# Token mixing of the first batch by one pair's 128 channels, with the first order, the merged order and the loads found anew

## The chip, the cores and the metric

The kernel runs on one core of a Trainium2 chip. The metric is the time of one execution on the device, in microseconds. The engines in play are TensorE (PE in the profile, with PEld for its weight loads), VectorE (DVE), ScalarE (ACT), GpSimd (POOL, which issues the loads) and SyncE (SP, which issues the first loads, the turning transfers and the stores).

## The reference

Attention with a sliding window of 128 and 4 sink positions, then a mixer: over tokens, then over channels.

```python
scores = scale * np.matmul(q, k.transpose(0, 1, 3, 2))       # 4 batches, 8 heads, 768 positions, 64 dims
is_sink = pos[None, :] < int(n_sink)
rel = pos[:, None] - pos[None, :]
keep = is_sink | ((rel >= 0) & (rel < int(window)))
scores = np.where(keep, scores, -1000000000.0)
...
x = np.ascontiguousarray(attn_out.transpose(0, 2, 1, 3)).reshape(B, S, H * D)     # 4 x 768 x 512
xt = x.transpose(0, 2, 1)
h = np.maximum(xt @ w_tok1, 0.0) @ w_tok2                     # 768 -> 256 -> 768, per channel
u = x + h.transpose(0, 2, 1)
h2 = np.maximum(u @ w_ch1, 0.0) @ w_ch2                       # 512 -> 1536 -> 512, per token
return (u + h2).astype(np.float32)
```

## The kernel before

*Units of work.* Two heads make a pair p; a batch b has four pairs (128 channels each), so there are 16 pairs, 0 to 15. q and k of a pair are turned (dims on the partitions): for pairs 0 to 7 by TensorE (`turn`, L473, and `transposed`, L491), for pairs 8 to 15 by a turning transfer that SP issues (`turned_by_dma`, L417). Scores of a pair are made in three groups g of two key tiles each (`scores`, L543), the exponential is ScalarE's (L583). What lies outside the window is removed in one of two ways. Either `masked` (L528) first writes -32768 into the bank by a matmul of the identity with a mask, so that the exponential gives zero; or VectorE multiplies the exponentials with a 0/1 mask afterwards (`mask`, L588). Batch 0 uses the first way for the (p, g) in `MASKED_BY_PE` (L69), which is all of its twelve groups but one. `pv` (L630) multiplies with the values, and VectorE takes the reciprocal and normalizes into x_sb.

*Token mixing* works on a group of channels (`group`, L733): here 256, so two groups, of two pairs each, per batch. `mix_h` (L752) makes relu(x w_tok1) for a group, with w_tok tiles as weights and 256 columns of x_sb streaming. `mix_u` (L780) makes the second product; the x that is added to it is either added by VectorE (L797) or, with `by_pe`, by a matmul of the identity into the same bank, after which ScalarE or VectorE copies. `transpose_u` (L862) turns u for batch 0 on TensorE in blocks of 128 x 128. In batch 0, mix_h takes one 128-row part at a time, and mix_u and transpose_u take two of the six token tiles.

*Channel mixing* of batch b (`mix_channels`, L968): 24 units v1(ft, half) of four matmuls of 384 columns each, whose weights are w_ch1 tiles and whose streaming operand is the turned u (uT); then for each of the six token tiles four `out_part` units of three 512-wide matmuls with w_ch2, an addition on VectorE (L1003) and a store. The first v1 unit of a half needs uT of all four pairs.

*The order* is set when the program is built, by a planner (class Plan, L266). It walks through three lists with estimated costs. FIRST_BATCH (L54) is the order of batch 0's attention and token mixing on TensorE, by short names: q0/k0 turns, m00 masks, s00 scores (pair, group), x1 sink scores, o00 values, h, u, t the token mixing. The main list is the channel mixing of all batches. The side list is the attention and token mixing of the next batch; MERGED (L47) gives, as n/m, which side unit n stands behind how many main units m. LOADS (L59) is the order in which GpSimd issues loads: v, q, k of a pair, T and A for w_tok1 and w_tok2, C0 to C3 for the quarters of w_ch1, D0 to D3 for those of w_ch2. Every engine then runs its own list in this order. q, k, v and weights are converted from float32 by the transfer. The planner keeps one estimate of the transfer queue (`queue`, L269), eight loads may be under way (LANES), and a turning transfer adds its `bulk` to the queue (L368). PSUM has two double banks for scores (ps_sc) and four banks for all else (ps_mx).

Of the kernel before, what the change touches and what calls it, by code (L numbers as in the profile page):

```python
# [10 lines left out]
BF16 = mybir.dt.bfloat16  # L11
# [5 lines left out]
def kernel(  # L17
# [15 lines left out]
    P = 128  # L33
# [13 lines left out]
    MERGED = (  # L47
# [5 lines left out]
    )  # L53
    FIRST_BATCH = (  # L54
        "q0 k0 m00 m01 s01 s00 q1 k1 m02 s02 m10 x1 s10 m11 q2 s11 o00 o01 m12 k2 s12 m20 s20 q3 m21 k3 s21 "
        "m22 o11 s22 o10 s30 x3 m31 h01 m32 s31 s32 o20 o21 h00 o30 o31 u02 u00 u04 h10 h11 t00 t02 t04 u10 "
        "u12 u14 t10 t12 t14"
    )
    LOADS = (  # L59
        "v1 v2 T0 v3 A0 q4 k4 v4 C0 C1 q5 k5 v5 q6 C2 q7 C3 k6 k7 D0 q8 D1 k8 v6 D2 D3 q9 v7 k9 q10 q11 k10 "  # L60
        "v8 k11 q12 v9 q13 v10 k12 k13 v11 k14 q14 q15 k15 v12 v13 v14 v15"
    )
# [5 lines left out]
    U_BY_DMA = [(2, 0), (2, 1), (3, 0), (3, 1)]  # L68
    MASKED_BY_PE = [(p, g) for p in range(NHP) for g in range(NT // 2) if (p, g) != (NHP - 1, 0)]  # L69

# [195 lines left out]
    class Plan:  # L266
        def __init__(self):
            self.free = {"PE": 0.0, "ACT": 0.0, "DVE": 0.0, "SP": 0.0, "POOL": 0.0}
            self.queue, self.landings = 0.0, []  # L269
# [69 lines left out]
        def run(self, first, main, side):  # L339
# [5 lines left out]
            while any(first) or main or side or self.pending:  # L345
# [13 lines left out]
                if o is not None and (t is None or o[0] <= t):  # L359
                    op = self.pending.pop(o[1])  # L360
                    op.fn(o[2])
                    self.free[o[2]] = o[0] + op.cost[o[2]]
                    op.done = self.free[o[2]] + op.lag
                    if op.loads:
                        self.queue = max(self.queue, self.free[o[2]] + FIRST) + op.lag
                        op.done = self.queue + LAND
                        self.landings += [op.done] * op.loads
                    elif op.bulk:  # L368
                        self.queue = max(self.queue, self.free[o[2]]) + op.bulk
                        if op.stores:  # L370
                            op.done = self.queue + LAND
                    continue
# [360 lines left out]
    def group(b, g):  # L733
        return g * DM // 2, DM // 2

# [5 lines left out]
    def u_part(b, g, s0, n):  # L741
        return tiles["mix", b][1].rearrange("p (g t c) -> p g t c", g=2, t=NT)[:, g, s0:s0 + n]

# [117 lines left out]

    def transpose_u(b, g, s0, n):  # L862
        ct0, nct = group(b, g)[0] // P, group(b, g)[1] // P
# [7 lines left out]
        w = nct * n * P  # L871
        op = Op(
            {"ACT": 190.0 + 0.78 * w, "DVE": 150.0 + 0.52 * w},
            lambda e: copy(
                e, tiles["mix", b][2].rearrange("c (g t k p) -> c g k t p", g=2, t=NT, p=P)[:, g, :, s0:s0 + n],
                tiles["ps_ut", b, g, s0].rearrange("c k (t p) -> c k t p", p=P),
            ),
        )
        op.urgent = 1 + g
        for half in range(s0 // QH, (s0 + n - 1) // QH + 1):  # L880
            done.setdefault(("uT", b, half), []).append(op)
        return unit(nct * n * 56, run, [done["u", b, g, s0]], {"mx": [[op]]}, [op])

    def first_attention():


        for p in range(NHP):
            prepare(p)
        made = {}
# [277 lines left out]
```

## Time and profile before

| | us |
|---|---|
| median of 3 runs (201.4 to 201.74) | 201.64 |
| profiled execution | 201.1 |
| its span | 199.3 |
| TensorE busy | 190.9 |
| ScalarE busy | 106.1 |
| VectorE busy | 99.7 |

How to read it: a profile row of a group has source line, engine, operation, output<-inputs, sizes and count, then busy time and the mean length of one in ns, then the idle time of the engine just before such an instruction and what ended it. A timeline row has start and length in us. Matmuls are pipelined: the length of one includes its fill, and the pace is read from the distance between starts. A transfer row gives the time from issue to landing. Line numbers of the changed kernel are lower by one to higher by four, depending on the place.

### The profile page before, as it was taken

Reading aid. Unit: us, or ns where it says so; the run is one execution under the profiler, and the core shown is the slowest. Engines: PE = TensorE matmul, PEld = TensorE weight load, DVE = VectorE, ACT = ScalarE, POOL = GpSimd, SP = SyncE. Lnnn points to the kernel's source line nnn. Section 1 sums busy time; section 2 is a strip of 40 time slices with the busy share of each in tenths; the row PEclk is TensorE's granted clock in tenths of the full one; section 3 lists DMA queues with packets and bytes.
Section 4 is the critical chain, followed back from the end, with each engine's and each line's share of the span. In section 5 each row is a group of like instructions: output and inputs, shape, how many; then the busy total and the mean of one; then the engine's idle time right before and its main releaser. Section 6 shows DMA issues by size and latency. Waiting matters only on the chain.

```text
span 199.3 us, 4761 instructions
## 1 busy us (share of the span) xinstructions
PE 190.9 (96%) x1997; PEld 114.6 (58%) x2015; DVE 99.7 (50%) x215; ACT 106.1 (53%) x185; POOL 67.9 (34%) x86
## 2 busy tenths in 40 slices
PE   6699999999999999999999999999999999999992
PEld 2355885566565665556556755656557746564452
DVE  4777763857867465326367676604235721001222
ACT  4899658988626225868556284776401106771000
POOL 6299869787547723648420000000000000000000
PEclk9999999999999999999999999999999999999999
DMA  6999999999999999999999845100021191000223
GB/s 205 291 258 185 168 183 171 176 183 180 162 150 131 169 150 226 148 208 151 158 155 165 204 103 135 54 2 3 0 99 62 32 230 53 3 0 9 96 109 105
DMA packets 92358, 26.28 MB, mean 132 GB/s; under 512 B 82352, under 2 KB 89392, under 8 KB 92336
## 3 DMA queue, kind: packets, MB, share of 16 engines
q0 software_dynamic: 67232, 11.80, 79.1%
q1 hardware_dynamic: 25104, 14.17, 32.2%
q8 instruction: 16, 0.26, 0.5%
q14 instruction: 6, 0.05, 0.1%
HBM read 26.75 MB, written 6.29 MB: 166 GB/s over the span
## 4 chain that ended last, share of the span: by engine, by line
PE 92%; DMA 3%; ACT 1%; issue 1%; SPq 1%; DVE 0%
PE ps_mx L135 83%; PE ps_sc L135 7%; DMA k_f<-in_k_dram 3%; PE ps_mx L483 1%; PE ps_sc L499 1%; SPq L107 1%; PE ps_mx L138 1%; PE ps_mx L471 0%; ACT pT L583 0%; ACT u_sb L142 0%; DVE k_bf L144 0%; ACT kT L142 0%; DVE o_sb L1041 0%
## 5 line engine op out<-in xcount | busy, mean ns | idle before, releaser
L135 PE MATMUL ps_mx<-w_ch,v1T 128*128 128x512 bf16 (+2 forms) x297 | 65.9, 362 | 0.9 <-issue 0.2
L135 PE MATMUL ps_mx<-uT,w_ch 128*128 128x384 bf16 x384 | 65.8, 326 | 0.0
L148 ACT ACTIVATE v1T<-ps_mx 128x384 bf16<-128x384 f32 x80 | 39.3, 492 | 26.7 <-PE ps_mx L135 14.2
L583 ACT ACTIVATE pT<-ps_sc 128x1024 bf16<-128x1024 f32 (+1 forms) x48 | 44.1, 951 | 12.9 <-PE ps_sc L135 11.6
L135 PEld LDWEIGHTS <-w_ch 128*128 128x128 bf16 x384 | 36.1, 98 | 24.1 <-DVE x_sb L693 0.5
L135 PEld LDWEIGHTS <-v1T 128*128 128x128 bf16 x312 | 28.3, 98 | 26.6 <-issue 0.2
L1003 DVE TENSOR_TENSOR o_sb<-ps_mx,u_sb 128x512 f32<-128x512 f32 x23 | 15.9, 689 | 38.3 <-PE ps_mx L135 32.4
L120 POOL DMA_DIRECT2D q_bf<-in_q_dram x24 | 19.8, 830 | 10.2 <-PE ps_mx L135 2.7
L120 POOL DMA_DIRECT2D k_bf<-in_k_dram x24 | 19.7, 826 | 5.3 <-DMA k_bf<-in_k_dram 3.0
L135 PEld LDWEIGHTS <-w_tok 128*128 128x128 bf16 x192 | 18.1, 98 | 4.8 <-issue 0.5
L128 POOL DMA_DIRECT2D v_aug<-in_v_dram x16 | 16.5, 1037 | 12.4 <-PE ps_mx L135 5.7
L150 DVE TENSOR_SCALAR v1T<-ps_mx 128x384 bf16<-128x384 f32 x16 | 8.8, 553 | 19.8 <-PE ps_mx L135 19.7
L797 DVE TENSOR_TENSOR u_sb<-ps_mx,x_sb 128x512 bf16<-128x512 f32 x21 | 13.8, 687 | 7.6 <-PE ps_mx L135 7.5
L135 PEld LDWEIGHTS <-pT 128*128 128x128 bf16 x352 | 14.5, 98 | 3.8 <-issue 0.3
L135 PE MATMUL ps_mx<-v_aug,pT 128*128 128x65 bf16 x352 | 15.7, 194 | 0.0
L148 ACT ACTIVATE h1T<-ps_mx 128x512 bf16<-128x512 f32 (+1 forms) x9 | 4.5, 503 | 20.8 <-PE ps_mx L135 20.7
L135 PE MATMUL ps_sc<-qT,kT 64*64 64x192 bf16 (+3 forms) x288 | 14.7, 249 | 0.1
L591 DVE TENSOR_TENSOR pT<-pT,mask_main 128x1024 bf16<-128x1024 bf16 (+1 forms) x24 | 14.1, 618 | 0.5 <-ACT pT L583 0.5
L135 PEld LDWEIGHTS <-kT 64*64 64x64 bf16 (+2 forms) x320 | 7.5, 101 | 10.7 <-issue 8.8
L135 PE MATMUL ps_mx<-h1T,w_tok 128*128 128x256 bf16 x96 | 13.2, 273 | 0.0
L135 PE MATMUL ps_mx<-x_sb,w_tok 128*128 128x256 bf16 x96 | 12.0, 273 | 0.1
L693 DVE TENSOR_TENSOR x_sb<-ps_mx,recip 128x384 bf16<-128x384 f32 x22 | 11.8, 551 | 0.2
(64 smaller groups left out, 119.1 us busy)
## 6 DMA issues: line engine op xcount, KB each, us to landing
out_dram<-o_sb SPq DMA_DIRECT2D x23, 256.0 KB, 2.8
v_aug<-in_v_dram POOLq DMA_DIRECT2D x16, 192.0 KB, 9.1
w_ch<-in_moe_w_ch_dram POOLq DMA_DIRECT2D x8, 384.0 KB, 7.7
q_bf<-in_q_dram POOLq DMA_DIRECT2D x24, 96.0 KB, 7.4
k_bf<-in_k_dram POOLq DMA_DIRECT2D x24, 96.0 KB, 8.4
q_f<-in_q_dram SPq DMA_DIRECT2D x4, 384.0 KB, 5.5
k_f<-in_k_dram SPq DMA_DIRECT2D x4, 384.0 KB, 6.0
w_tok<-in_moe_w_tok_dram POOLq DMA_DIRECT2D x2, 384.0 KB, 7.5
```

The lines of the kernel that those rows point to most:

```text
L107: in_order(nc.sync.dma_start(out=f, in_=rows_of(pidx, n).rearrange("p h j d -> p h (j d)")))
L120: in_order(nc.gpsimd.dma_start(out=out[:, h], in_=rows[:, h]))
L128: in_order(nc.gpsimd.dma_start(out=v_aug.rearrange("p i t d -> p (i t) d")[:, :, 0:D], in_=v[b].rearrange("h s d -> (h s) d")[2 * hp * S:2 ...
L135: in_order(nc.tensor.matmul(*args, skip_group_check=True, **kwargs))
L138: in_order(nc.tensor.transpose(out, in_, ident))
L148: in_order(nc.scalar.activation(out, in_, AF.Relu))
L150: in_order(nc.vector.tensor_scalar_max(out=out, in0=in_, scalar1=0.0))
L583: in_order(nc.scalar.activation(part(tiles["pT", p][:, :, ds(2 * g, 2)]), of_keys(tiles["ps_s", p, g])[:, :, 0:width(g)], AF.Exp, scale=scale,
L591: in_order(nc.vector.tensor_tensor(out=pt, in0=pt, in1=m, op=ALU.mult))
L693: in_order(nc.vector.tensor_tensor(out=x_sb[b][:, :, ds((2 * hp + i) * D, D)], in0=tiles["ps_o", p, i][:, :, 0:D], in1=tiles["recip", p, i ...
L797: in_order(nc.vector.tensor_tensor(out=u_part(b, g, s0, n), in0=tiles["ps_u", b, g, s0], in1=x_sb[b][:, s0:s0 + n, c0:c0 + cn], op=ALU.add,))
L1003: in_order(nc.vector.tensor_tensor(out=o_sb.rearrange("p (g c) -> p g c", g=2), in1=u_rows(b, st), in0=tiles["ps_out", b, st].rearrange("p ...
```

## The change

- Token mixing of batch 0 works by one pair: `group` gives 128 channels for b == 0, so four groups instead of two. mix_h makes both 128-row parts of a pair in one bank (2 x 128 columns), mix_u and transpose_u take three token tiles of one pair (3 x 128 columns). Additions, copies and relus change their sizes with it.
- The identity is added by TensorE for two of the eight mix_u units of 3 x 128 columns (named y01 and y30), before for three of six units of 2 x 256.
- FIRST_BATCH is a new order; a mask unit is made only where it is named. It names nine of the twelve: m20 and m22 are gone beside m30, and VectorE multiplies these groups with a mask.
- The planner lets a turning transfer delay the loads that are still under way, by half of its `bulk` each. This is in the planner's estimates alone.
- MERGED is a new order, and LOADS is new from its sixth name on. Sets of transfers, of side units and of channel mixing are the same.

```diff
     FIRST_BATCH = (
-        "q0 k0 m00 m01 s01 s00 q1 k1 m02 s02 m10 x1 s10 m11 q2 s11 o00 o01 m12 k2 s12 m20 s20 q3 m21 k3 s21 "
-        "m22 o11 s22 o10 s30 x3 m31 h01 m32 s31 s32 o20 o21 h00 o30 o31 u02 u00 u04 h10 h11 t00 t02 t04 u10 "
-        "u12 u14 t10 t12 t14"
+        "q0 k0 m00 s00 m01 s01 q1 m02 k1 s02 m11 x1 s11 m10 q2 s10 o01 m12 k2 s12 o00 m21 q3 s21 s20 k3 o11 "
+        "s22 x3 o10 m31 s30 s31 o20 h0 m32 o21 s32 h1 o30 o31 y01 u00 h2 u10 u11 t00 h3 u20 t01 t11 y30 t10 "
+        "u21 t20 t30 u31 t31 t21"
     )
     LOADS = (
-        "v1 v2 T0 v3 A0 q4 k4 v4 C0 C1 q5 k5 v5 q6 C2 q7 C3 k6 k7 D0 q8 D1 k8 v6 D2 D3 q9 v7 k9 q10 q11 k10 "
-        "v8 k11 q12 v9 q13 v10 k12 k13 v11 k14 q14 q15 k15 v12 v13 v14 v15"
+        "v1 v2 T0 v3 A0 k4 q4 C0 q5 C1 k5 q6 C2 k6 v4 v5 D0 q7 k7 C3 q8 v6 k8 D1 D2 D3 v7 q9 k9 v8 k10 v9 q10 "
+        "v10 k11 q11 q12 q13 k12 k13 v11 k14 v12 q14 v13 v14 k15 q15 v15"
     )
...
-    MASKED_BY_PE = [(p, g) for p in range(NHP) for g in range(NT // 2) if (p, g) != (NHP - 1, 0)]
...
                         self.landings += [op.done] * op.loads
+                        self.loading.append((op, len(self.landings) - op.loads))
                     elif op.bulk:
                         self.queue = max(self.queue, self.free[o[2]]) + op.bulk
+                        for load, n in self.loading:
+                            if load.done > o[0] + LAND:
+                                load.done += 0.5 * op.bulk
+                                self.landings[n:n + load.loads] = [load.done] * load.loads
...
     def group(b, g):
-        return g * DM // 2, DM // 2
+        cn = P if b == 0 else DM // 2
+        return g * cn, cn
...
-    def transpose_u(b, g, s0, n):
+    def transpose_u(b, ct, s0, n):
         def run():
-            ps_ut = tiles["ps_ut", b, g, s0] = bank("mx", nct, n * P, dtype=BF16)
-            for ct in range(nct):
-                for st in range(n):
-                    transpose(ps_ut[:, ct, ts(st, P)], u_part(b, g, s0 + st, 1)[:, 0, ts(ct, P)])
+            ps_ut = tiles["ps_ut", b, ct, s0] = bank("mx", n, P, dtype=BF16)
+            for st in range(n):
+                transpose(ps_ut[:, st], u_part(b, ct, s0 + st, 1)[:, 0])
...
-                if (p, g) in MASKED_BY_PE:
+                if f"m{p}{g}" in names:
                     made[f"m{p}{g}"] = masked(p, g)
...
-        for g in range(2):
-            for t in range(NTOK):
-                made[f"h{g}{t}"] = mix_h(0, g, t, 1)
-            for st in range(0, NT, 2):
-                made[f"u{g}{st}"] = mix_u(0, g, st, 2, (g, st) in [(0, 2), (1, 2), (1, 4)])
-            for st in range(0, NT, 2):
-                made[f"t{g}{st}"] = transpose_u(0, g, st, 2)
-        return [[made[name] for name in FIRST_BATCH.split()]]
+        for ct in range(NC):
+            made[f"h{ct}"] = mix_h(0, ct, 0, NTOK)
+            for half in range(2):
+                by_pe = f"y{ct}{half}" in names
+                made["uy"[by_pe] + f"{ct}{half}"] = mix_u(0, ct, half * QH, QH, by_pe)
+                made[f"t{ct}{half}"] = transpose_u(0, ct, half * QH, QH)
+        return [[made[name] for name in names]]
```

The beginnings of the two merged orders (side unit / main units ahead of it) and their ends:

```diff
-        "0/0 1/2 2/4 3/8 7/11 4/16 6/17 5/17 8/20 10/22 9/22 11/24 12/24 16/26 14/26 17/27 13/30 15/30 18/30 "
+        "0/0 1/2 2/3 3/8 7/11 4/15 5/16 6/18 8/19 9/20 10/20 11/22 12/23 13/25 15/25 16/27 14/27 18/27 17/27 "
...
-        "60/132 70/133 63/133 61/133 62/134 72/134 71/135 73/135"
+        "62/126 66/128 68/128 69/129 70/132 71/134 72/135 73/135"
```

More of the change, by code (lines that the diff above doesn't have):

```diff
@@ L268, in __init__ @@
             self.free = {"PE": 0.0, "ACT": 0.0, "DVE": 0.0, "SP": 0.0, "POOL": 0.0}
-            self.queue, self.landings = 0.0, []
+            self.queue, self.landings, self.loading = 0.0, [], []
             self.half = False
@@ L741, in u_part @@
     def u_part(b, g, s0, n):
-        return tiles["mix", b][1].rearrange("p (g t c) -> p g t c", g=2, t=NT)[:, g, s0:s0 + n]
+        c0, cn = group(b, g)
+        half, c = divmod(c0, DM // 2)
+        return tiles["mix", b][1].rearrange("p (g t c) -> p g t c", g=2, t=NT)[:, half, s0:s0 + n, c:c + cn]
     def u_rows(b, st):
@@ L860, in transfer_u @@
             plan.pending.append(op)
-    def transpose_u(b, g, s0, n):
-        ct0, nct = group(b, g)[0] // P, group(b, g)[1] // P
+    def transpose_u(b, ct, s0, n):
         def run():
-            ps_ut = tiles["ps_ut", b, g, s0] = bank("mx", nct, n * P, dtype=BF16)
-            for ct in range(nct):
-                for st in range(n):
-                    transpose(ps_ut[:, ct, ts(st, P)], u_part(b, g, s0 + st, 1)[:, 0, ts(ct, P)])
-        w = nct * n * P
+            ps_ut = tiles["ps_ut", b, ct, s0] = bank("mx", n, P, dtype=BF16)
+            for st in range(n):
+                transpose(ps_ut[:, st], u_part(b, ct, s0 + st, 1)[:, 0])
         op = Op(
-            {"ACT": 190.0 + 0.78 * w, "DVE": 150.0 + 0.52 * w},
+            {"ACT": 190.0 + 0.78 * n * P, "DVE": 150.0 + 0.52 * n * P},
             lambda e: copy(
-                e, tiles["mix", b][2].rearrange("c (g t k p) -> c g k t p", g=2, t=NT, p=P)[:, g, :, s0:s0 + n],
-                tiles["ps_ut", b, g, s0].rearrange("c k (t p) -> c k t p", p=P),
+                e, tiles["mix", b][2].rearrange("c (g t k p) -> c g k t p", g=2, t=NT, p=P)[:, ct // 2, ct % 2, s0:s0 + n],
+                tiles["ps_ut", b, ct, s0],
             ),
         )
-        op.urgent = 1 + g
+        op.urgent = 1 + ct / 2
         for half in range(s0 // QH, (s0 + n - 1) // QH + 1):
             done.setdefault(("uT", b, half), []).append(op)
-        return unit(nct * n * 56, run, [done["u", b, g, s0]], {"mx": [[op]]}, [op])
+        return unit(n * 56, run, [done["u", b, ct, s0]], {"mx": [[op]]}, [op])
     def first_attention():
@@ L888, in first_attention @@
             prepare(p)
-        made = {}
+        made, names = {}, FIRST_BATCH.split()
         for p in range(NHP):
```

6 rows, old and new, of the table MERGED are left out of this document.

## The prediction

> **What bounds the kernel now.** I read the page's busy totals and chain first, then the busy times by stage, then the timelines of TensorE and ScalarE in the first 30 us, last the loads.
>
> ```profile
> PE 190.9 (96%) x1997; PEld 114.6 (58%) x2015; DVE 99.7 (50%) x215; ACT 106.1 (53%) x185; POOL 67.9 (34%) x86
> ...
> PE 92%; DMA 3%; ACT 1%; issue 1%; SPq 1%; DVE 0%
> ```
>
> TensorE holds 92% of the chain that ended last. The table by stage shows where it is idle (columns: stretch, its length, then busy time and count of PE, PEld, DVE, ACT, POOL, granted clock, DMA share, GB/s):
>
> ```profile
> 8.00:23.00 15.00, 13.88 (x251) 8.78 (x255) 10.80 (x26) 13.76 (x20) 13.72 (x17) 1.00 1.84 214
> 23.00:30.00 7.00, 6.75 (x86) 5.89 (x84) 5.15 (x12) 3.31 (x7) 5.20 (x7) 1.00 1.81 180
> 30.00:60.00 30.00, 29.89 (x384) 18.41 (x385) 20.05 (x42) 21.96 (x40) 22.04 (x28) 1.00 1.85 170
> 60.00:190.00 130.00, 129.26 (x1194) 75.70 (x1206) 57.39 (x114) 62.77 (x114) 23.67 (x27) 1.00 0.91 107
> ```
>
> From 30 to 190 us TensorE is idle for 0.11 + 0.74 = 0.85 us, so after 30 us only less work on it, or a new wait, moves the end. From 8 to 30 us it is idle for 1.12 + 0.25 = 1.37 us. In the stretch from 8 to 23 us ScalarE is as full as TensorE (13.76 against 13.88 of 15 us): its exponentials turn banks over there, and that is where the change takes matmuls out. The whole change lies in these first 30 us, plus the order of side work and loads later. The clock is 1.00 throughout and is no term.
>
> The profiled execution took 201.1 us (span 199.3 and 1.8 around it), the median of the runs is 201.64. I sum against 201.1 and add 0.54 at the end.
>
> **The change, part by part.** TensorE rows of the first 30 us (start, length, instruction, count):
>
> ```profile
> 7.96 0.35 PE L483 MATMUL ps_mx<-ident,q_bf 64*128 64x64 bf16 x12 [0.25 <-DVE q_bf L144]
> 9.00 0.35 PE L483 MATMUL ps_mx<-ident,k_bf 64*128 64x64 bf16 x12 [0.70 <-DVE k_bf L144]
> ...
> 11.17 0.60 PE L135 MATMUL ps_sc<-mask_add,ident 128*128 128x512 bf16 x2
> 11.71 0.35 PE L483 MATMUL ps_mx<-ident,q_bf 64*128 64x64 bf16 x12
> ...
> 16.19 0.50 PE L135 MATMUL ps_sc<-mask_add,ident 128*128 128x384 bf16 x2
> 16.53 0.22 PE L135 MATMUL ps_mx<-v_sink,pT_sink 128*128 128x130 bf16 x1
> ...
> 23.03 0.27 PE L135 MATMUL ps_mx<-x_sb,ident 128*128 128x256 bf16 x1
> 23.14 0.38 PE L135 MATMUL ps_mx<-h1T,w_tok 128*128 128x256 bf16 x2
> ...
> 24.55 1.47 PE L135 MATMUL ps_mx<-x_sb,w_tok 128*128 128x256 bf16 x12
> 25.86 0.83 PE L138 MATMUL ps_mx<-ident,u_sb 128*128 128x128 bf16 x12
> 26.53 0.60 PE L135 MATMUL ps_mx<-h1T,w_tok 128*128 128x256 bf16 x4
> ...
> 29.75 1.47 PE L135 MATMUL ps_mx<-uT,w_ch 128*128 128x384 bf16 x8
> ```
>
> Lengths here contain the fill, so I price by the distance from start to start.
>
> 1. *Two masks leave TensorE* (m20, m22 are no longer named in the order of the first batch). A pair of 512-wide ones occupies 11.17 to 11.71, 0.54; a pair of 384-wide ones 16.19 to 16.53, 0.34. Together -0.88.
>
> 2. *Identity matmuls.* Six of 256 columns become six of 128. One of 256 takes 23.03 to 23.14, 0.11. The twelve 128-wide transposes, each with its own weight load, take 25.86 to 26.53, 0.056 each. 6 x (0.056 - 0.11) = -0.32.
>
> 3. *Mixing by pairs.* 48 matmuls of 256 columns (24 of the first product, 24 of the second) become 96 of 128, with 48 more weight loads. Twelve 256-wide ones take 24.55 to 25.86, 0.109 each. 96 x 0.056 - 48 x 0.109 = +0.15. The other row of this width is:
>
> ```profile
> L135 PE MATMUL ps_mx<-w_ch,v1T 128*128 128x128 bf16 x24 | 1.5, 219 | 0.0
> L138 PEld LDWEIGHTS <-u_sb 128*128 128x128 bf16 x24 | 1.5, 98 | 0.5 <-ACT u_sb L142 0.4
> ```
>
> 1.5 / 24 = 0.0625, with the fill of two groups in it, would make it +0.77. I take +0.15, from the row with the same rhythm (new weights for each 128 columns), and keep +0.77 as an end. The 24 transposes of u stay 24.
>
> A rule speaks against this part. The Trainium skill, "TensorE: Matmul & The Clock Gate", section "Back-to-back issue gap", gives a sustained spacing of about 81 ns for 128-wide matmuls that each load weights. By it this part would be 96 x 0.081 - 48 x 0.109 = +2.5 us, an estimate from that page, and the whole change would lose 1.3 us. The trace does not agree at the nearest row: 56 ns.
>
> 4. *The masks return on VectorE*, as two multiplications behind their exponentials:
>
> ```profile
> L591 DVE TENSOR_TENSOR pT<-pT,mask_first 128x1024 bf16<-128x1024 bf16 x13 | 8.8, 673 | 3.4 <-ACT pT L583 3.4
> L591 DVE TENSOR_TENSOR pT<-pT,mask_main 128x768 bf16<-128x768 bf16 x12 | 6.6, 552 | 0.0
> ```
>
> 0.67 + 0.55 = 1.22 us more. VectorE is busy 10.80 of the 15 us, so it has 4.2 us to take it; but the multiplications now stand ahead of the normalization of pairs 1 and 2, which the mixing waits for. Hidden by the scores of pair 3 and the other halves: 0. If that cover is gone: up to +1.22. The smaller evictions (six additions and eight copies of 384 columns in place of six and six of 512) are off the path for the same reason.
>
> 5. *New order of the first batch.* m02 now stands between the two turns of pair 1, and its 0.34 fills half of the 0.70 in which TensorE waits for k of pair 1; s00 runs before m01, so the first exponential can start sooner. Against that, fewer matmuls are left to cover waits for exponentials. ScalarE's rows:
>
> ```profile
> 7.53 1.94 ACT L583 ACTIVATE pT<-ps_sc 128x1024 bf16<-128x1024 f32 x2 [0.43 <-PE ps_sc L135]
> ...
> 20.50 1.73 ACT L583 ACTIVATE pT<-ps_sc 128x1024 bf16<-128x1024 f32 x2 [0.27 <-PE ps_sc L135]
> ```
>
> Twelve exponentials run almost without a gap from 7.53 to 22.23, and their number doesn't change. Bounds: -0.95 (both waits of 0.25 and 0.70 filled) and +0.88 (all that the masks free comes back as waits for ScalarE). I take 0: gaps are filled at one end of that chain and opened at the other.
>
> 6. *Later loads.* The set of loads decides when one lands, since the queue is full. The last quarter of the first channel weight (C3 in the list) moves from behind q7 to behind v4, v5, D0, q7 and k7. Up to it the new list holds exactly the fifteen loads that the old one holds up to D0, so it lands when D0 lands now. POOL's issue of D0, its time to landing, and TensorE around the first use of C3:
>
> ```profile
> 36.87 0.74 POOL L153 DMA_DIRECT2D w_ch<-in_moe_w_ch_dram  x1 [0.48 <-DMA w_ch<-in_moe_w_ch_dram]
> 43.73 1.62 POOL L153 DMA_DIRECT2D w_ch<-in_moe_w_ch_dram  x2
> ```
> ```profile
> w_ch<-in_moe_w_ch_dram POOLq DMA_DIRECT2D x1, 384.0 KB, 7.4
> ...
> w_ch<-in_moe_w_ch_dram POOLq DMA_DIRECT2D x1, 384.0 KB, 10.8
> ```
> ```profile
> 44.92 2.17 PE L135 MATMUL ps_mx<-uT,w_ch 128*128 128x384 bf16 x12
> 47.03 0.35 PE L499 MATMUL ps_sc<-ident,q_bf 64*128 64x64 bf16 x12
> ```
>
> D0 lands at 36.87 + 7.4 = 44.3. C3 is needed by the second of the three v1 units that start at 44.92, at 44.92 + 2.11 / 3 = 45.6; the same units stand ahead of it in the new order, so it comes at 45.6 - 1.05 = 44.5. The margin is 0.2 us: 0, with an open end. D1 to D3 land last in a set of 21 loads that is the same in both lists; the last, issued about 44.5, took 10.8 and lands at 55.3, while the first output tile that needs it is added at 57.4:
>
> ```profile
> 57.39 0.69 DVE L1003 TENSOR_TENSOR o_sb<-ps_mx,u_sb 128x512 f32<-128x512 f32 x1 [0.23 <-PE ps_mx L135]
> ```
>
> Its three matmuls (0.65) begin near 56.5: 1.2 us to spare. If C3 took 10.8 as that one, it would land 3.4 us later and stall TensorE for 3.2.
>
> 7. *SP's queue, POOL's, and the merged order.* The counts of transfers, stores and side units stay; turns of pairs 8 and 9 now all stand ahead of the first store. A store waiting behind a turn delays an o_sb buffer, of which there are six, and so an addition on VectorE. Cost 0, hidden behind TensorE's queue; ends -0.85 (all idle time from 30 to 190 us gone) and +0.85 (it doubles).
>
> Sum: -0.88 - 0.32 + 0.15 = -1.05, so 200.05 for the profiled execution, and 200.6 for the median.
>
> **The rivals.**
>
> *The first batch is paced by ScalarE and VectorE, so what TensorE is spared there becomes waiting.* For it: 13.76 of 15 us on ScalarE, and 1.22 us more on VectorE. Against it: the last exponential ends at 22.23, the first v1 matmul starts at 29.75, and in between TensorE is idle for 0.25 us; two of four mixing products now stand ahead of pair 3's last rows, and fill waits. Price: +0.88 back, -1.05 + 0.88 = -0.17, so 201.4: no change to be measured.
>
> *C3 comes late* (the other side). For it: the margin of 0.2 us, and w_ch landings that stretch from 7.4 to 10.8 us under load. Against it: the 10.8 came with a turning transfer in flight, and the first of these is issued at 45.7, after C3 should have landed:
>
> ```profile
> 45.73 1.32 SPq L426 DMA_TRANSPOSE qT<-q_bf  x1
> ```
>
> It decides from 1.65 us of delay on (1.05 + 0.4 + the margin). At the full 3.4: -1.05 + 3.2, so 203.8; at half of it 202.1.
>
> *Weight loads show.* If the 48 added loads were not hidden, at 1.5 / 24 = 0.0625 each, +3.0: 203.6. Against it: the transposes' 56 ns. The rule of the Trainium skill that part 3 names is this case, in a milder size.
>
> *More is gained*: the waits of 0.95 us go too, 199.7.
>
> **How the numbers follow.** A measurement of this kernel tells about 0.2%, 0.4 us, from no change. The sum as it stands: 0.55. ScalarE's pace: 0.17, of which half falls under 0.2%. C3 or another load late: 0.20. Weight loads: 0.04. More: 0.04. Faster is 0.55 + 0.04 + part of the second, less the forecast's own upper edge, 0.63; same 0.15; slower 0.22. The likeliest case's own range is 200.0 to 201.2 (half of part 4's end to either side). The range of 8 in 10 goes from 199.8, below which is only the gain of all waits, to 202.5, which takes in ScalarE's pace and a C3 late by half the stretch.
>
> **What would show it.** Right: the first v1 matmul at about 28.4 to 28.8 instead of 29.75 (six transposes of u, 0.34 us, now stand behind it), TensorE's total near 189.9, two more multiplications with the mask, 128-wide mixing at 56 ns from start to start, idle time of at most 0.9 us from 30 to 190 us. Wrong: a wait of TensorE for a w_ch load near 44.5 or 54; idle time from 8 to 23 us that grows from 1.12 towards 2; waits of TensorE for x_sb near 22; 128-wide groups at 80 ns or more; ScalarE or VectorE standing for a v_aug landing while v1 evictions queue behind.

## The result, and the profile after

The changed kernel takes 200.4 us (median of 7 runs, 199.74 to 201.35), the kernel before beside it 201.74 us (7 runs, 201.4 to 202.21): a ratio of 0.9936, with a 95% interval of 0.9916 to 0.9956, so 1.3 us less, between 0.9 and 1.7. Ratios are made of fast executions alone: of the kernel with the new first batch and the old later orders, five of twelve were slow (205.0 to 206.0 us at a granted clock of 0.992) and are left out. The profiled execution took 200.4 us (span 198.6), the one of before 201.1 (span 199.3).

The page's busy totals and the chain of the changed kernel:

```profile
PE 191.5 (96%) x2041; PEld 115.5 (58%) x2059; DVE 101.8 (51%) x224; ACT 105.5 (53%) x182; POOL 68.0 (34%) x86
...
PE 90%; POOL 4%; DMA 3%; DVE 1%; issue 1%; SPq 1%; POOLq 0%
```

TensorE has 44 more matmuls and 44 more weight loads than before, and its busy time has not fallen but risen by 0.6 us. So as far as the records tell, the gain is not less work on TensorE. (Both traces have 18 matmuls fewer than weight loads, 1997 for 2015 and 2041 for 2059: some records are missing, so a busy total is a little too small.) The busy times of the changed kernel by stage (stretch, length, then busy time and count of PE, PEld, DVE, ACT, POOL, granted clock, DMA share, GB/s):

```profile
8.00:23.00 15.00, 14.11 (x252) 8.64 (x253) 12.14 (x27) 13.54 (x20) 12.81 (x16) 1.00 1.68 223
23.00:30.00 7.00, 7.00 (x131) 6.51 (x128) 5.69 (x14) 3.87 (x9) 6.11 (x8) 1.00 1.80 181
30.00:60.00 30.00, 29.89 (x389) 18.63 (x388) 21.66 (x49) 21.22 (x36) 21.23 (x26) 1.00 1.86 172
60.00:190.00 130.00, 129.16 (x1195) 76.02 (x1206) 56.51 (x113) 62.85 (x112) 24.48 (x29) 1.00 0.90 108
```

From 23 to 30 us TensorE no longer waits (7.00 of 7.00, before 6.75). To see what this is worth I cut both spans at three events: the end of the last normalization of batch 0, the turn of q of pair 5 (the first turn into a score bank), and the start of the last addition into o_sb. Ahead of the second event the changed kernel has three v1 units where the kernel before has four, so one unit is added (0.65 us, four matmuls of 384 columns, by the starts 29.34 and 30.00 below). The first two events, before and then after:

```profile
23.61 0.56 DVE L654 TENSOR_TENSOR x_sb<-ps_mx,recip 128x384 bf16<-128x384 f32 x1
32.84 0.35 PE L499 MATMUL ps_sc<-ident,q_bf 64*128 64x64 bf16 x12
```
```profile
24.07 0.56 DVE L658 TENSOR_TENSOR x_sb<-ps_mx,recip 128x384 bf16<-128x384 f32 x1
32.12 0.35 PE L503 MATMUL ps_sc<-ident,q_bf 64*128 64x64 bf16 x12
```

| us | before | after | difference |
|---|---|---|---|
| to the end of the last normalization | 24.17 | 24.63 | +0.46 |
| from there to the turn of q of pair 5 (after: 32.12 - 24.63 + 0.65) | 8.67 | 8.14 | -0.53 |
| from there to the last addition (after: 195.59 - 32.12 - 0.65) | 162.87 | 162.82 | -0.05 |
| from the start of the last addition to the end of the span | 3.59 | 3.01 | -0.58 |
| sum: the span | 199.3 | 198.6 | -0.7 |

Two stretches got shorter. The first row is the head, which varies from execution to execution: over the profiles of this study the normalization ended between 24.17 and 25.63, and the kernel before, which showed the 24.17, sits at the short end. The +0.46 can't be put down to the change: in this execution of the changed kernel two 512-wide mask matmuls near 8 us still took 0.97 us (7.73 to 8.70), in that of one kernel of the experiments with the same attention (without identity matmuls, with earlier loads) 0.53 (6.96 to 7.49).

*The second row, on TensorE.* The timeline of the kernel before, behind the normalization, has four identity matmuls (27.95 is the last) and a wait of the last four transposes for ScalarE's copy of u:

```profile
26.97 0.27 PE L135 MATMUL ps_mx<-x_sb,ident 128*128 128x256 bf16 x1
...
27.95 0.27 PE L135 MATMUL ps_mx<-x_sb,ident 128*128 128x256 bf16 x1
...
29.14 0.40 PE L138 MATMUL ps_mx<-ident,u_sb 128*128 128x128 bf16 x4 [0.24 <-ACT u_sb L142]
```

The same stretch of the changed kernel:

```profile
24.32 0.83 PE L134 MATMUL ps_mx<-x_sb,w_tok 128*128 128x128 bf16 x12
24.98 0.83 PE L134 MATMUL ps_mx<-h1T,w_tok 128*128 128x128 bf16 x12
...
27.16 0.22 PE L134 MATMUL ps_mx<-x_sb,ident 128*128 128x128 bf16 x1
...
28.59 0.50 PE L134 MATMUL ps_mx<-h1T,w_tok 128*128 128x128 bf16 x6
29.02 0.39 PE L487 MATMUL ps_mx<-ident,q_bf 64*128 64x64 bf16 x12
29.34 0.82 PE L134 MATMUL ps_mx<-uT,w_ch 128*128 128x384 bf16 x4
30.00 0.50 PE L137 MATMUL ps_mx<-ident,u_sb 128*128 128x128 bf16 x6
```

The twelve 128-wide matmuls at 24.32 take until 24.98: 55 ns each. The kernel before has about 27.5 mixing matmuls of 256 columns left behind its normalization, at 0.109 each 3.0 us; the changed one has 54 of 128 columns, at 0.055 also 3.0 us. What differs is the identity, 4 x 0.11 = 0.44 before and 3 x 0.055 = 0.17 after, and the wait of 0.24, which is gone because the last six transposes (30.00) now stand behind a v1 unit. Together 0.51 of the 0.53 us, as priced from these rows.

*The fourth row, the stores at the end.* Before (the DMA view of the window 192 to 205 us, then VectorE's and SP's last rows):

```profile
q8 instruction: 1, 0.02, 0.7%
...
out_dram<-o_sb SPq DMA_DIRECT2D x1, 256.0 KB, 3.3
out_dram<-o_sb SPq DMA_DIRECT2D x1, 128.0 KB, 2.6
out_dram<-o_sb SPq DMA_DIRECT2D x2, 64.0 KB, 1.7
```
```profile
194.82 2.13 SPq L1046 DMA_DIRECT2D out_dram<-o_sb  x3
...
195.71 0.29 DVE L1041 TENSOR_TENSOR o_sb<-ps_mx,u_sb 128x128 f32<-128x128 f32 x1 [0.38 <-PE ps_mx L135]
```

After:

```profile
out_dram<-o_sb SPq DMA_DIRECT2D x1, 256.0 KB, 2.0
out_dram<-o_sb SPq DMA_DIRECT2D x1, 128.0 KB, 1.7
out_dram<-o_sb SPq DMA_DIRECT2D x2, 64.0 KB, 1.6
```
```profile
194.70 1.54 SPq L1048 DMA_DIRECT2D out_dram<-o_sb  x3
...
195.59 0.29 DVE L1043 TENSOR_TENSOR o_sb<-ps_mx,u_sb 128x128 f32<-128x128 f32 x1 [0.38 <-PE ps_mx L134]
```

The same three stores of the last token tile land faster, and SP needs 1.54 us to issue them instead of 2.13. The one thing in the window that is there before and not after is the row "q8 instruction": a transfer of 16 KB of program. Both kernels have 16 of them in all; in the kernel before the last falls among the last stores, in the changed one it comes 9 us earlier. The experiments return to this.

*The last quarter of w_ch1.* GpSimd's issue, its landing, and TensorE at the first unit that needs it, in the changed kernel:

```profile
37.07 0.77 POOL L152 DMA_DIRECT2D w_ch<-in_moe_w_ch_dram  x1
```
```profile
w_ch<-in_moe_w_ch_dram POOLq DMA_DIRECT2D x1, 384.0 KB, 8.0
```
```profile
45.51 0.81 PE L134 MATMUL ps_mx<-uT,w_ch 128*128 128x384 bf16 x4
```

It lands at 37.07 + 8.0 = 45.1, 0.4 us ahead of 45.51, and TensorE does not wait for it.

### The profile page after: what moved, and what is told of

Same layout as the page of the kernel before. It is cut to its first block, busy times and chain, and to the rows that moved or that the text cites. A ratio compares the mean times of both kernels' runs of the same rounds, so it can differ in the third digit from the quotient of the medians.

```text
span 198.6 us, 4863 instructions
## 1 busy us (share of the span) xinstructions
PE 191.5 (96%) x2041; PEld 115.5 (58%) x2059; DVE 101.8 (51%) x224; ACT 105.5 (53%) x182; POOL 68.0 (34%) x86
## 4 chain that ended last, share of the span: by engine, by line
PE 90%; POOL 4%; DMA 3%; DVE 1%; issue 1%; SPq 1%; POOLq 0%
PE ps_mx L134 82%; PE ps_sc L134 5%; DMA v_sink_f<-in_v_dram 3%; POOL v_aug L127 2%; POOL w_tok L152 1%; PE ps_mx L137 1%; PE ps_sc L503 1%; SPq L213 1%; PE ps_mx L487 0%; PE ps_mx L475 0%; POOL k_bf L143 0%; POOL q_bf L143 0%; POOL v_sink L143 0%; DVE v_sink_f L209 0%; DVE mask_add L178 0%
## 5 line engine op out<-in xcount | busy, mean ns | idle before, releaser
L134 PE MATMUL ps_mx<-uT,w_ch 128*128 128x384 bf16 x384 | 66.6, 326 | 0.0
L134 PE MATMUL ps_mx<-w_ch,v1T 128*128 128x512 bf16 (+2 forms) x297 | 65.2, 362 | 0.9 <-issue 0.3
L134 PEld LDWEIGHTS <-w_tok 128*128 128x128 bf16 x240 | 19.5, 98 | 4.8 <-issue 0.2
L804 DVE TENSOR_TENSOR u_sb<-ps_mx,x_sb 128x512 bf16<-128x512 f32 (+1 forms) x24 | 15.2, 655 | 13.1 <-PE ps_mx L134 13.1
L595 DVE TENSOR_TENSOR pT<-pT,mask_main 128x768 bf16<-128x768 bf16 (+1 forms) x25 | 14.7, 615 | 1.3 <-ACT pT L587 1.2
L134 PE MATMUL ps_mx<-h1T,w_tok 128*128 128x256 bf16 (+1 forms) x120 | 13.9, 252 | 0.1
L134 PE MATMUL ps_mx<-x_sb,w_tok 128*128 128x256 bf16 (+1 forms) x120 | 12.2, 251 | 0.0
```

Of the source, the lines that this page charges most:

```text
L134: in_order(nc.tensor.matmul(*args, skip_group_check=True, **kwargs))
L595: in_order(nc.vector.tensor_tensor(out=pt, in0=pt, in1=m, op=ALU.mult))
L804: in_order(nc.vector.tensor_tensor(out=u_part(b, g, s0, n), in0=tiles["ps_u", b, g, s0], in1=x_sb[b][:, s0:s0 + n, c0:c0 + cn], op=ALU.add,))
```

## The experiments

The theory on record gave the gain to TensorE: two masks and the identity's columns less. The rivals: ScalarE paces the first batch, so that the masks are worth nothing; a late load takes it back. The first experiments do one part of the change alone, or all but one.

**The two masks alone.** The kernel before, with these two masks on VectorE:

```diff
-        "q0 k0 m00 m01 s01 s00 q1 k1 m02 s02 m10 x1 s10 m11 q2 s11 o00 o01 m12 k2 s12 m20 s20 q3 m21 k3 s21 "
-        "m22 o11 s22 o10 s30 x3 m31 h01 m32 s31 s32 o20 o21 h00 o30 o31 u02 u00 u04 h10 h11 t00 t02 t04 u10 "
+        "q0 k0 m00 m01 s01 s00 q1 k1 m02 s02 m10 x1 s10 m11 q2 s11 o00 o01 m12 k2 s12 s20 q3 m21 k3 s21 "
+        "o11 s22 o10 s30 x3 m31 h01 m32 s31 s32 o20 o21 h00 o30 o31 u02 u00 u04 h10 h11 t00 t02 t04 u10 "
...
-    MASKED_BY_PE = [(p, g) for p in range(NHP) for g in range(NT // 2) if (p, g) != (NHP - 1, 0)]
+    MASKED_BY_PE = [(p, g) for p in range(NHP) for g in range(NT // 2) if (p, g) not in ((NHP - 1, 0), (2, 0), (2, 2))]
```

> The kernel before, with the masks of groups (2, 0) and (2, 2) moved from TensorE to VectorE and nothing else. If TensorE's work decides (the sum of the prediction): 0.88 us less than before, a ratio near 0.9955. If ScalarE and VectorE pace the first batch: at most 0.2 us less, a ratio of 0.999 or more, and TensorE's idle time from 8 to 23 us grows by what the masks took.

202.15 us, a ratio of 1.001 (0.9983 to 1.0036): no change, and -0.88 us (0.9956) is excluded. Its busy times from 8 to 23 us:

```profile
8.00:23.00 15.00, 13.10 (x236) 8.08 (x237) 11.62 (x26) 13.66 (x21) 13.01 (x16) 1.00 1.71 210
```

TensorE's busy time there fell from 13.88 to 13.10, nearly what the two masks took, and ScalarE stayed at 13.66: the freed time is idle time. Two waits for ScalarE stand there that the kernel before does not have, one for its copy of a turned k and one for an exponential:

```profile
14.90 0.39 PE L135 MATMUL ps_sc<-qT,kT 64*128 64x256 bf16 x4 [0.41 <-ACT kT L142]
18.34 0.40 PE L135 MATMUL ps_sc<-qT,kT 64*128 64x256 bf16 x4 [0.27 <-ACT pT L583]
```

**The change with the two masks back.**

```diff
-        "q0 k0 m00 s00 m01 s01 q1 m02 k1 s02 m11 x1 s11 m10 q2 s10 o01 m12 k2 s12 o00 m21 q3 s21 s20 k3 o11 "
-        "s22 x3 o10 m31 s30 s31 o20 h0 m32 o21 s32 h1 o30 o31 y01 u00 h2 u10 u11 t00 h3 u20 t01 t11 y30 t10 "
+        "q0 k0 m00 s00 m01 s01 q1 m02 k1 s02 m11 x1 s11 m10 q2 s10 o01 m12 k2 s12 o00 m21 q3 s21 m20 s20 k3 o11 "
+        "m22 s22 x3 o10 m31 s30 s31 o20 h0 m32 o21 s32 h1 o30 o31 y01 u00 h2 u10 u11 t00 h3 u20 t01 t11 y30 t10 "
```

> The changed kernel, with these two masks back on TensorE. If TensorE's work decides: 0.88 us more than the changed kernel, a ratio to before near 0.998. If ScalarE and VectorE pace the first batch: the changed kernel's ratio of 0.9936, within 0.001.

200.35 us, a ratio of 0.9926 (0.9899 to 0.9952): as fast as the change itself. Both ways the masks are worth nothing that can be measured.

**The later orders alone.** The kernel before, with the new MERGED, LOADS and planner:

```diff
+                        for load, n in self.loading:
+                            if load.done > o[0] + LAND:
+                                load.done += 0.5 * op.bulk
...
-        "v1 v2 T0 v3 A0 q4 k4 v4 C0 C1 q5 k5 v5 q6 C2 q7 C3 k6 k7 D0 q8 D1 k8 v6 D2 D3 q9 v7 k9 q10 q11 k10 "
+        "v1 v2 T0 v3 A0 k4 q4 C0 q5 C1 k5 q6 C2 k6 v4 v5 D0 q7 k7 C3 q8 v6 k8 D1 D2 D3 v7 q9 k9 v8 k10 v9 q10 "
...
```

> The kernel before with the new merged order, the new loads and the planner's delay of loads; first order and mixing as before. If the later lists are worth nothing by themselves (the prediction's parts 6 and 7): a ratio of 1.000 within 0.0015. If the gain is theirs: near 0.994.

202.09 us, 1.0014 (0.9986 to 1.0043): nothing. Its second stretch is 8.66, its third 162.82, its end 3.65.

**The new first batch with the old later orders.** The inverse of the edit before, on the changed kernel.

> The changed kernel with the old merged order, the old loads and the planner as before; first order and mixing are the new ones. If the gain is TensorE's work in the first batch: a ratio near 0.994, like the changed kernel. If the later lists bring it: near 1.000. A third case, that the old lists don't fit the earlier start (loads late by up to 1 us): 0.997 with a wait of TensorE for a load.

The ratio is 0.9971 (0.9933 to 1.0008), an interval that holds both the ratio of the change and no change, so the median does not tell how much of the gain needs the new lists. The profile shows what they are for:

```profile
PE ps_sc L499 <- DMA k_bf<-in_k_dram: 0.6, 1, 0.6
```

The second stretch is short (8.15) and the end too, but TensorE, which arrives earlier, waits 0.6 us for a k load of the old list, and the third stretch takes 163.64.

**Mixing by pairs with the old order of the attention, and the other way round.** Two kernels that split FIRST_BATCH, both with the new later lists. One has the old attention with all eleven masks, and the new mixing:

```diff
+        "q0 k0 m00 m01 s01 s00 q1 k1 m02 s02 m10 x1 s10 m11 q2 s11 o00 o01 m12 k2 s12 m20 s20 q3 m21 k3 "
+        "s21 m22 o11 s22 o10 s30 x3 m31 h0 m32 s31 s32 o20 o21 h1 o30 o31 y01 u00 h2 u10 u11 t00 h3 u20 t01 "
...
```

> The changed kernel with the attention of the first batch in the old order (all eleven masks named); mixing by pairs, merged order and loads are the new ones. The theory after the first four runs: TensorE's masks are worth nothing, and half of the gain comes from mixing by pairs, half from the order of the attention. By it: from the last normalization of batch 0 to the turns of pair 5, with one v1 unit (0.65 us) added for the different place of that burst, 8.1 us instead of 8.67, while from the cast of k of pair 3 to that normalization it stays at 9.4 us; a ratio near 0.997. Rival one, the order of the attention does it all: 8.7 and 9.4 us, a ratio of 1.000. Rival two, mixing by pairs does it all: a ratio of 0.994.

The other has the new attention with nine masks, and mixes by halves of 256 channels:

```diff
+        "q0 k0 m00 s00 m01 s01 q1 m02 k1 s02 m11 x1 s11 m10 q2 s10 o01 m12 k2 s12 o00 m21 q3 s21 s20 k3 "
+        "o11 s22 x3 o10 m31 s30 s31 o20 h01 m32 o21 s32 h00 o30 o31 u02 u00 u04 h10 h11 t00 t02 t04 u10 u12 u14 "
...
```

> The kernel before with the attention of the first batch in the new order (nine masks), and the new merged order and loads; mixing stays in groups of 256 channels. By the theory: 8.9 us from the cast of k of pair 3 to the last normalization instead of 9.4, and 8.7 us from there to the turns of pair 5; a ratio near 0.997. Rival one (the order does it all): 0.994. Rival two (mixing does it all): 1.000.

With pairs: 200.89 us, 0.9956 (0.9935 to 0.9978). With halves: 202.03 us, 1.0006 (0.998 to 1.0032). The half of the gain that the theory gave to the order of the attention did not come: the new mixing carries the gain that can be measured. The new mixing is three things at once, though: units of one pair, fewer identity columns, and more instructions on TensorE. The second stretch is 8.14 with pairs and 8.66 with halves; the end is 3.0 and 4.1. Over all profiles of this study the second stretch splits in this way (8.66 to 8.67 in four kernels with halves, 8.14 to 8.20 in five with pairs that keep the identity matmuls).

**The last quarter of w_ch1 one place later.**

```diff
-        "v1 v2 T0 v3 A0 k4 q4 C0 q5 C1 k5 q6 C2 k6 v4 v5 D0 q7 k7 C3 q8 v6 k8 D1 D2 D3 v7 q9 k9 v8 k10 v9 q10 "
+        "v1 v2 T0 v3 A0 k4 q4 C0 q5 C1 k5 q6 C2 k6 v4 v5 D0 q7 k7 q8 C3 v6 k8 D1 D2 D3 v7 q9 k9 v8 k10 v9 q10 "
```

> The changed kernel with the last quarter of the first channel weight one place later, behind q of pair 8. If the margin is as small as the changed kernel's trace has it (landing 45.1 us, first use 45.5 us): the load lands 1.3 us later and TensorE waits 0.9 us for it, a ratio near 0.998. If the load is not on the path: no wait, the changed kernel's ratio.

202.03 us, 0.9996 (0.9962 to 1.003): by the median the whole gain is gone by one place in the queue. TensorE at the first use:

```profile
47.41 0.82 PE L134 MATMUL ps_mx<-uT,w_ch 128*128 128x384 bf16 x4 [1.20 <-DMA w_ch<-in_moe_w_ch_dram]
```

The margin is nearly as thin as the prediction said; the rival was real and lies one place away. (In this profile the third stretch is 1.9 us longer than with the change; the wait is 1.2 of it.)

**Without the identity matmuls.** The changed kernel, with the x of all units added by VectorE:

```diff
-        "s22 x3 o10 m31 s30 s31 o20 h0 m32 o21 s32 h1 o30 o31 y01 u00 h2 u10 u11 t00 h3 u20 t01 t11 y30 t10 "
+        "s22 x3 o10 m31 s30 s31 o20 h0 m32 o21 s32 h1 o30 o31 u01 u00 h2 u10 u11 t00 h3 u20 t01 t11 u30 t10 "
```

> The changed kernel without the six identity matmuls: VectorE adds x in all eight units. By the prediction's second term TensorE has 0.34 us less to do: from the last normalization to the turns of pair 5 7.2 us instead of 7.5 (as the rows stand, no unit added). If VectorE is what the last units wait for: 7.8 us or more, with idle time of TensorE between 23 and 30 us.

200.57 us, 0.9922 (0.9892 to 0.9952), not to be told from the change. From the end of the last normalization to the turn it now takes 7.60 us, 0.54 less. Most of that is the event and not TensorE: VectorE makes one of the new additions just ahead of the last normalization, which so ends later.

```profile
24.05 0.56 DVE L804 TENSOR_TENSOR u_sb<-ps_mx,x_sb 128x384 bf16<-128x384 f32 x1
24.53 0.55 DVE L658 TENSOR_TENSOR x_sb<-ps_mx,recip 128x384 bf16<-128x384 f32 x1
```

An event on TensorE itself is the first value matmul of pair 3, in the changed kernel and then in this one:

```profile
22.57 0.35 PE L134 MATMUL ps_mx<-v_aug,pT 128*128 128x65 bf16 x6
```
```profile
22.61 0.35 PE L134 MATMUL ps_mx<-v_aug,pT 128*128 128x65 bf16 x6
...
32.04 0.35 PE L503 MATMUL ps_sc<-ident,q_bf 64*128 64x64 bf16 x12
```

From there to the turn the change takes 32.12 - 22.57 = 9.55 us and this kernel 9.43: only 0.12 less, where the six identity matmuls at 0.055 were priced at 0.33. Why the rest did not come is not shown. (By the same two events the kernel before takes 10.72 us and the change, with 0.65 added, 10.20; the half microsecond of the table above stands.) The third stretch rises by 0.8 to 163.64, where two waits appear:

```profile
PE ps_mx L134 <- DVE v1T L149: 0.4, 1, 0.4
...
PE ps_sc L503 <- DMA k_bf<-in_k_dram: 0.2, 1, 0.2
```

Ahead of the first of them VectorE stands 2.43 us for a value load, with the relu of a v1 unit behind it; in the changed kernel it stands 1.55 us there and TensorE does not wait. The missing identity matmuls need not be the reason: the kernel with the two masks back, which has the loads and the mixing of the change, shows the same (VectorE 2.79 us, TensorE 0.74, a third stretch of 163.62).

**The same with earlier loads.** The fifth value load moves ahead of three loads, and the last quarter of w_ch1 changes places with the first of w_ch2:

```diff
-        "v1 v2 T0 v3 A0 k4 q4 C0 q5 C1 k5 q6 C2 k6 v4 v5 D0 q7 k7 C3 q8 v6 k8 D1 D2 D3 v7 q9 k9 v8 k10 v9 q10 "
+        "v1 v2 T0 v3 A0 k4 q4 C0 q5 C1 k5 v4 q6 C2 k6 v5 C3 q7 k7 D0 q8 v6 k8 D1 D2 D3 v7 q9 k9 v8 k10 v9 q10 "
```

> The changed kernel without the two identity matmul groups (the second half of each of these pairs writes its own tile of mixed channels), and with the fifth value load and the last quarter of w_ch1 two or one places earlier in the queue. Theory (without the identity matmuls the stretch from the last normalization of the first batch to the turn of pair 5 takes 7.6 instead of 8.14 us, and what was lost behind it was two late loads): that stretch stays at 7.6, the stretch from there to the last addition is back from 163.64 at 162.8 to 163.0, and the time is 0.5 us below the changed kernel, a ratio of 0.991 or less. Rival (the later stretch gives it back in any order of the loads): 163.4 or more there, and a ratio of 0.993 to 0.994.

200.33 us, 0.9908 (0.988 to 0.9937), the span of the profile 198.0. The second stretch stays at 7.60 and the third is back at 162.88. VectorE no longer stands for a value load there, and TensorE's busy time behind the first batch is full:

```profile
30.00:60.00 30.00, 30.00 (x399) 18.45 (x400) 21.16 (x46) 21.03 (x38) 20.71 (x25) 1.00 1.86 170
60.00:190.00 130.00, 130.00 (x1204) 75.95 (x1197) 57.20 (x115) 62.45 (x110) 24.65 (x29) 1.00 0.90 108
```

So in this profile the earlier loads take the waits away. That they make the kernel faster is not shown: the interval overlaps that of the change (0.9916 to 0.9956) and that of the kernel without the earlier loads. The span is 0.6 us below that of the change, but 0.53 of it lies ahead of the first value matmul of pair 3 (22.04 against 22.57), in the head, which varies by more than that.

**And the cast of k of pair 3 ahead of the token weights.** This kernel is the one before it with one edit more. In the changed kernel TensorE waits 0.4 us for this cast on GpSimd, behind an issue of w_tok2:

```diff
+            done["tok2"].deps.append(done["k_bf", NHP - 1])
```

> The same as the kernel without identity matmuls and with earlier loads, and the second load of the token weights is issued only after GpSimd's cast of k of pair 3, which it held up. Theory (TensorE's 0.4 us wait for that cast is on the path of the first batch): the wait is gone and the time falls by up to 0.4 us more, a ratio of about 0.989. Rival (ScalarE's exponentials set the pace there): no change against the kernel without it, or a loss if the token weights come later than the first mixing needs them.

199.99 us, but over 5 runs: 0.9892 (0.984 to 0.9944), which tells nothing apart from the kernel without this edit. The wait for GpSimd is gone from the profile; another one, for k of pair 0, which landed late and was cast on VectorE, covers any effect there, and so does the granted clock, which this profile has at 0.57 from 8 to 12 us:

```profile
PE ps_mx L487 <- DVE k_bf L143: 1.9, 1, 1.9
```

Inconclusive.

**The store tail.** In the first four kernels with halves that were profiled, a program transfer fell between 192 us and the end, and the last row of the table was 3.6 to 4.1 us; in the first six with pairs there was none and it was 3.0 to 3.1. Pairs or program length? The kernel before, with its warm-up matmuls of 512 columns each in eight pieces. The profile counts 7 of them, each with a weight load, so 14 instructions (not 14 matmuls, as the expectations below have it); in pieces they are 56 and 56, so 98 TensorE instructions more for the same columns:

```diff
-            mm(ps, ones[:, 0:P], ones, start=True, stop=True)
+            for c in range(8):
+                mm(ps[:, ts(c, 64)], ones[:, 0:P], ones[:, ts(c, 64)], start=True, stop=True)
```

> The kernel before with 98 more TensorE instructions and no other work: each of the 14 warm-up matmuls of 512 columns at its head is done in eight pieces of 64 columns. Theory (the code transfer of 16 KB that meets the kernel before's last stores is shifted by the count of TensorE's instructions): with 98 more, as the changed kernel has 88 more, the transfer comes some 9 us earlier, at about 185 us of the span; the last 256, 128 and 64 KB stores land in 2.0, 1.7 and 1.6 us; the last addition to the end of the span takes 3.0 to 3.1 us instead of 3.6; the time is 0.5 to 0.6 us below the kernel before, a ratio of about 0.997. Rival (the shorter tail belongs to mixing by pairs, or to chance): the tail stays at 3.6 or more and the ratio is 1.000, or above it if the warm-up itself takes longer.

No program transfer is left in the window, and the stores land as in the changed kernel:

```profile
out_dram<-o_sb SPq DMA_DIRECT2D x2, 256.0 KB, 2.0
out_dram<-o_sb SPq DMA_DIRECT2D x1, 128.0 KB, 1.7
out_dram<-o_sb SPq DMA_DIRECT2D x2, 64.0 KB, 1.6
```
```profile
195.38 1.54 SPq L1047 DMA_DIRECT2D out_dram<-o_sb  x3
...
196.27 0.29 DVE L1042 TENSOR_TENSOR o_sb<-ps_mx,u_sb 128x128 f32<-128x128 f32 x1 [0.38 <-PE ps_mx L135]
```

The end is 199.3 - 196.27 = 3.0 with mixing by halves. The median, 201.79 us, gives 0.9988 (0.9954 to 1.0022), which holds both -0.6 us and nothing. (The warm-up did not become dearer on TensorE, but the head of this execution was 0.57 us longer than that of the kernel before.)

The counterpart: the changed kernel with 168 TensorE instructions more, 256 more than the kernel before (the change itself has 44 matmuls and 44 weight loads more). Beside the warm-up with its 98, its mask matmuls are cut into 35 more, each with a weight load:

```diff
-                mm(
-                    of_keys(ps)[:, i, 0:width(g)], ident,
-                    mask_adds[g == 0].rearrange("p k n q -> p (k n q)")[:, 0:width(g)], start=True, stop=False,
-                )
+                n = 2 if (p, g, i) == (3, 2, 1) else 3
+                for c in range(n):
...
+                    mm(
+                        of_keys(ps)[:, i, c0:c0 + w], ident,
+                        mask_adds[g == 0].rearrange("p k n q -> p (k n q)")[:, c0:c0 + w], start=True, stop=False,
+                    )
```

This changes the computation: cut in this way, the mask matmuls do not leave the full mask in the scores of the first batch, so its values differ from the reference's; the counts, widths and waits are the intended ones.

> The changed kernel with 168 more TensorE instructions and no other work: the 14 warm-up matmuls in eight pieces each, and each mask matmul of the first batch in three pieces (one of them in two). That is 256 more than in the kernel before, so that a code transfer should come at the same place of the program as there. Theory (code transfer): the last addition to the end of the span takes 3.6 to 4.1 us again instead of 3.0, and the time is 0.5 to 0.6 us above the changed kernel, a ratio of about 0.9966 to the kernel before. Rival: the tail stays at 3.0 to 3.1 and the ratio at 0.994.

A seventeenth program transfer appears at the end, and the stores slow down again:

```profile
q8 instruction: 1, 0.02, 0.7%
...
out_dram<-o_sb SPq DMA_DIRECT2D x1, 256.0 KB, 3.4
out_dram<-o_sb SPq DMA_DIRECT2D x1, 128.0 KB, 2.6
out_dram<-o_sb SPq DMA_DIRECT2D x2, 64.0 KB, 2.1
```

The end is 199.4 - 196.07 = 3.3: half of the expected 0.6 us. The ratio to the kernel before, 0.9945 (0.9913 to 0.9977), can't be told from that of the change. So it is shown that TensorE's instruction count decides whether a program transfer meets the last stores, and that they then land slower; that this is worth 0.3 to 0.6 us is read from single profiles, and no median has confirmed it: moving the transfer away from the kernel before gave 0.2 us, with an interval from 0.9 less to 0.4 more.

## Why the prediction was right, and where it was not

The forecast of 200.6 us and the measured 200.4 agree, but the gain is made of other parts than the sum had. That the two numbers are so close is in good part luck: the largest term, the masks, brought nothing, and a shorter end of the span and a wait that went away, which the sum did not have, took its place. Point by point:

- *Two masks leave TensorE, -0.88.* This step failed, and it was most of the sum. Taken out alone they gave nothing (1.001), put back they cost nothing. The rival that ScalarE paces the first batch described this term rightly: taken out alone, the masks left idle time on TensorE from 8 to 23 us (1.90 us, before 1.12), with two waits for ScalarE in it. I had set it at 0.17 because I looked at TensorE's small idle time behind 23 us, not at the engine whose work the masks stand beside.
- *Identity matmuls, -0.32.* Right in kind by the rows: 0.27 of it can be counted behind the normalization. But the price is not what a stretch gains each time: the six that are left were priced at 0.33, and without them TensorE was 0.12 us faster. No kernel here has pairs with the old number of identity columns, so how the 0.53 us divide between the two is priced, not shown.
- *Mixing by pairs, +0.15.* The price per matmul was right, 55 ns against 56. The Trainium skill, "TensorE: Matmul & The Clock Gate", section "Back-to-back issue gap", has 81 ns for this rhythm; the trace does not agree, and the loss that followed from it did not come. What the step lacked is the wait of 0.24 us for ScalarE's copy of u, which is gone because the last six transposes now stand behind a v1 unit; the prediction saw it as idle time and left it out of the sum.
- *Masks on VectorE, 0.* Right: VectorE goes from 10.80 to 12.14 us of 15, and in the kernel that changes this alone nothing is slower.
- *New order of the first batch, 0.* Right as far as can be measured: with halves the new order gives 1.0006. In the profile TensorE's waits for k moved from VectorE (1.3 before, 0.4 after) to GpSimd (0.4).
- *Later loads, 0 with a margin of 0.2.* Right, and the most useful line of the prediction: landing and first use both came later than forecast (45.1 and 45.5 us, for 44.3 and 44.5), so the margin was 0.4 us, and one place later cost 1.20 us of waiting and all of the gain.
- *SP's queue and the merged order, 0.* Right for the third stretch (162.87 and 162.82). But the ends of 0.85 rested on idle time that is none: the kernel before with the cut warm-up shows 30.00 of 30 and 130.00 of 130 us busy and the same 162.86 us. Its trace has a matmul for each weight load, 2064, and that of the kernel before 18 too few, so the 0.85 were records missing from the trace.
- *Not in the sum at all:* the end of the span, -0.58 in the profile. By the profile the two found terms, -0.53 and -0.58, make -1.1; the measured -1.3 (0.9 to 1.7) holds that. The first is in every profile with pairs, the second follows TensorE's instruction count, but its size is not confirmed by a median, so up to that much of the gain has no shown cause.

Of what was to be seen: the first v1 matmul stands at 29.34, not at 28.4 to 28.8 (0.46 of that is the longer head); TensorE's total rose to 191.5 instead of falling to 189.9, though missing records blur both totals; the 55 ns and the absence of a wait for w_ch came as said. One sign of being wrong was there, without harm in this profile: VectorE stood 1.55 us for a value load with the relu of a v1 unit behind it.

## What to carry to other kernels

Price work that is taken off an engine by what its neighbours do in that stage: where two engines are about equally full, as TensorE and ScalarE here (13.88 and 13.76 of 15 us), less work on one can become idle time and nothing else. Cut the span at a few events that every version has and compare the stretches; here that showed in one table that the gain lay in a stretch of 8 us and in the last 3 us, while busy totals pointed elsewhere. Check that an edit has not moved the event itself: one more addition on VectorE ahead of the last normalization made a stretch look 0.54 us shorter, where TensorE had gained 0.12. When an early stage gets shorter, look at once at the loads behind it, because 0.4 us of margin is soon used up.

## What the runs showed of the hardware

- A 16 KB transfer of program that falls among the last stores slows them: 256, 128 and 64 KB land in 3.3, 2.6 and 1.7 us instead of 2.0, 1.7 and 1.6, and SP's issue of three stores takes 2.13 us instead of 1.54. Where it falls depends on the number of TensorE's instructions: 98 more moved it out of the last microseconds, and 256 more than in the kernel before brought one back to the same place. The Trainium skill, "Runtime: NRT & Kernel Launch", section "Instruction fetch mechanics", has blocks of 16 KB with 256 instructions, and calls the cost of crossing one mostly hidden; the trace agrees with the blocks (16 transfers of 0.26 MB in all, and one more with 256 instructions more) and shows a place where the cost is not hidden.
- A matmul of 128 columns with its own weight load costs 55 ns and one of 256 columns 109 ns in these streams, so halving the width of the mixing cost nothing, at twice the number of weight loads.
- The head of the kernel, up to the last normalization of the first batch, varied by 1.5 us between profiled executions (24.17 to 25.63). Two things differ in the rows: when the first loads land (the cast of k of pair 0 begins at 5.22 us in the kernel before and at 6.40 in the slowest head), and the pace of the first matmuls: of the 512-wide masks near 6 us, four take 0.97 us in the kernel before (6.12 to 7.09), and two do in the changed one (6.22 to 7.19), both under a granted clock of 1.00 in the profile. What sets that pace is not shown. A difference of a few tenths there in a pair of profiles says nothing.
